# One computed order for the operations behind the softmax, on five queues

## The chip, the cores and the metric

The kernel runs on one core of a Trainium2 chip. The metric is the device time of one execution in microseconds (us); the kernel before takes 1281.55 us, the median of three runs (1279.1 to 1284.47). TensorE does the matrix products (PE; PEld is its weight load), VectorE (DVE) and ScalarE (ACT) work elementwise, GpSimd (POOL) does a little elementwise work, and SyncE (SP) issues the transfers. Each engine works through a queue of its own in a fixed order, and an instruction waits there for results of other engines.

## The reference

Channel attention over 6016 tokens of 256 channels is followed by two feed-forward networks. In short:

```
qn, kn = q / norm over tokens, k / norm over tokens
a = softmax(kn^T qn / tau)                  # 256 x 256
x = v @ a                                   # 6016 x 256
h = x @ w_in                                # network 1, 2048 wide
g = h where h >= 1; 0 where h <= -1; else (h + 1)^2 / 4
x = g @ w_out
xn = x / sqrt(mean(x^2) + 1e-6) * rms_g     # network 2, 1536 wide
out = (silu(xn @ w_gate) * (xn @ w_val)) @ w_out2
```

q, k and v are float32. The five weight matrices arrive as 64-bit floats.

## The kernel before

**Stages.** First q and k are read, their scores are summed up on TensorE, and the softmax gives the 256 x 256 matrix a. It is multiplied into w_in (`product_a`, four parts of 512 columns), so that network 1 works on v directly. Behind the softmax the 6016 tokens are treated as twelve tiles in six pairs: ten tiles of 512 tokens and two of 448. A pair goes through network 1 and later through network 2, in the order 1(0), 1(1), 2(0), 1(2), 2(1), 1(3), 2(2), 1(4), 2(3), 1(5), 2(4), 2(5), where 1(q) is network 1 of pair q.

**Precision.** Each operand of a product is split in a high part (h) and the rest (l), a ScalarE copy and a VectorE subtraction, and a product is three matmuls: high by high, low by high, high by low.

**Network 1.** For a tile t and a slice f of 128 of the 2048 columns, `emit_A` issues six matmuls into a PSUM tile h, `start_g` and `finish_g` turn it into gh and gl (three ScalarE and two VectorE instructions), and `block_B` adds it to the result y with six matmuls. A pair has 32 such blocks. `norm` and `combine` then normalize y, with two small matmuls into ms for each tile, and make the seven operands for network 2.

**Network 2.** The two tiles of a pair and the two halves of the channels form a 2 x 2 block product, done with seven products instead of eight. A group p covers 256 of the 1536 columns: seven products with w_gate (PSUM tiles gx, gz, gy), seven with w_val (vx, vz, vy), three matmuls each. Four products of a set go into the same accumulator, gx or vx; after the first three, ScalarE copies the sum so far out (ga, gc, gu and va, vc, vu, line 773) before the next product adds to it, and VectorE adds gz, gy, vz or vy to the copies (line 778). After the fourth, the sum is used straight from PSUM: ScalarE takes the Silu of the gate part (812), VectorE multiplies (818), uh and ul are split off, and `block_D` multiplies them with w_out2 into o. D is put off by one group: eight units of three matmuls of the group before are mixed in. A group thus has 22 units of three matmuls. `GROUP` is the order of units in it, written by hand: g, v and d stand for the next product of each set and a unit of D. There are four PSUM tiles for h, ms and the products, and two larger ones for y and o.

**Weights.** A 64-bit weight tile is read (wide), narrowed to float32 by bit operations on VectorE and ScalarE (`narrow`: clamp 223, shift 228 or 230, sign 234, rescale 238, join 242), and split. For w_in that serves `product_a`; w_out, w_gate, w_val and w_out2 are stored converted in DRAM (kept) and read again for each pair (wo, gw, vw, wd). For w_gate and w_val the seven weight combinations are formed, four of them by GpSimd (279), split by ScalarE (282) and VectorE (284). There are 34 such conversions; they run beside network 1 of pairs 0 and 1, so many steps after each block (`convert`, `pump`). Three tiles hold gw and vw.

**What sets the order.** The program is traced in loop order; a scheduler then places the instructions of each engine after estimated times, with priorities given in the code (`tc.high_priority`). TensorE's order behind the first 32 blocks is held as traced (`in_order(ENG.PE)`, line 941). Buffers come from pools that hand out the oldest free tile. `network_1` starts the norms of the pair before (task steps, two after each block); `network_2` starts the v tiles for a later pair. `store` transposes o and issues four stores for each half tile on SyncE (870).

## Time and profile before

| | |
|---|---|
| median of three runs | 1281.55 us (1279.1 to 1284.47) |
| the profiled execution's own time | 1281.39 us |
| its span, first to last instruction | 1279.6 us |
| TensorE busy | 1165.7 us, 4950 matmuls |
| VectorE busy | 850.1 us, 1311 instructions |
| ScalarE busy | 763.4 us, 1325 instructions |
| GpSimd busy | 80.1 us |
| granted TensorE clock, mean share of full | 0.985 |

The page gives the totals of one profiled execution; views of its trace give the busy time of each engine in any stretch, the instructions in order of time, and for each wait the instruction that ended it. The ends of matmuls are modelled, and matmuls overlap, so their start times tell more than their durations. Idle time of an engine that nothing waits for costs nothing.

### The profile page before, as it was taken

How to read it: one execution, taken by the hardware profiler on the slowest of the kernel's cores; microseconds unless marked ns; L12 is line 12 of the kernel's file. 1: busy time of each engine (PE TensorE's matmuls, PEld its weight loads, DVE VectorE, ACT ScalarE, POOL GpSimd, SP SyncE). 2: the span in 40 equal slices, each digit the busy share in tenths (PEclk: the TensorE clock that was granted, in tenths of full speed). 3: DMA queues.
4: the chain of work that ended last, by engine and by line, in shares of the span. 5: the costliest groups of instructions: out<-in, count | busy, mean ns of one | idle time of the engine just before them, and what ended most of it. 6: DMA issues, size and time to landing. Idle time of an engine off the chain costs nothing.

```text
span 1279.6 us, 13966 instructions
## 1 busy us (share of the span) xinstructions
PE 1165.7 (91%) x4950; PEld 927.0 (72%) x4950; DVE 850.1 (66%) x1311; ACT 763.4 (60%) x1325; POOL 80.1 (6%) x84
## 2 busy tenths in 40 slices
PE   8899987898999998999998999998999998889896
PEld 7677755676668786777786767786667897667775
DVE  6898889856558756557756556756556856765554
ACT  7687887774446665445675445666445765554442
POOL 0000334300001000000000000000000100100000
PEclk9989998999999999999999999999999999999998
DMA  9945786515334114344114444112334212433631
GB/s 355 223 138 156 279 295 238 158 54 134 142 137 122 50 50 117 138 148 132 42 50 119 148 141 115 66 50 91 107 144 138 80 50 91 148 120 132 179 133 29
DMA packets 138854, 167.65 MB, mean 131 GB/s; under 512 B 103712, under 2 KB 103712, under 8 KB 138784
## 3 DMA queue, kind: packets, MB, share of 16 engines
q1 hardware_dynamic: 138784, 166.75, 40.9%
q8 instruction: 39, 0.64, 0.2%
q14 instruction: 31, 0.25, 0.1%
HBM read 142.21 MB, written 24.51 MB: 130 GB/s over the span
## 4 chain that ended last, share of the span: by engine, by line
PE 48%; DVE 22%; ACT 18%; issue 4%; DMA 3%; POOL 2%; SPq 1%; DVEq 0%; ACTq 0%; POOLq 0%
PE o L851 12%; PE vx L760 8%; PE h L606 7%; PE gx L760 6%; PE y L649 6%; DVE g L617 5%; ACT gh L142 4%; ACT g L616 4%; PE gy L760 3%; ACT g L615 3%; DVE va L778 2%; PE vz L760 2%; DVE va L818 2%; DVE gl L139 2%; ACT vc L773 2%
## 5 line engine op out<-in xcount | busy, mean ns | idle before, releaser
L649 PE MATMUL y<-gh,wo 128*128 128x512 f32 (+1 forms) x768 | 237.7, 391 | 5.1 <-ACT gh L142 4.9
L142 ACT ACTIVATE gh<-g 128x512 fp32r<-128x512 f32 (+1 forms) x192 | 119.4, 622 | 121.9 <-DVE g L617 121.8
L139 DVE TENSOR_TENSOR gl<-g,gh 128x512 fp32r<-128x512 f32 (+1 forms) x192 | 134.5, 701 | 76.7 <-ACT gh L142 75.7
L851 PE MATMUL o<-uh,wd 128*128 128x512 f32 (+1 forms) x576 | 176.6, 388 | 0.0
L649 PEld LDWEIGHTS y<-gh,wo 128*128 128x128 f32 x768 | 144.5, 190 | 37.2 <-ACT gh L142 10.9
L617 DVE SCALAR_TENSOR_TENSOR g<-h,g 128x512 f32<-128x512 f32 (+1 forms) x192 | 129.6, 675 | 54.5 <-ACT g L616 53.4
L649 PE MATMUL y<-gl,wo 128*128 128x512 f32 (+1 forms) x384 | 151.5, 394 | 11.6 <-DVE gl L139 11.3
L606 PE MATMUL h<-vh,w1h 128*128 128x512 f32 (+1 forms) x384 | 150.6, 392 | 3.3 <-DVE g L617 3.0
L606 PE MATMUL h<-vl,w1h 128*128 128x512 f32 (+1 forms) x384 | 149.6, 390 | 0.0
L851 PEld LDWEIGHTS o<-uh,wd 128*128 128x128 f32 x576 | 108.6, 188 | 21.0
L616 ACT ACTIVATE g<-g 128x512 f32<-128x512 f32 (+1 forms) x192 | 119.5, 622 | 5.4
L606 PE MATMUL h<-vh,w1l 128*128 128x512 f32 (+1 forms) x384 | 119.1, 390 | 0.0
L851 PE MATMUL o<-ul,wd 128*128 128x512 f32 (+1 forms) x288 | 112.0, 389 | 0.0
L615 ACT ACTIVATE g<-h 128x512 f32<-128x512 f32 (+1 forms) x192 | 109.9, 572 | 0.7 <-PE h L606 0.5
L649 PEld LDWEIGHTS y<-gl,wo 128*128 128x128 f32 x384 | 72.6, 189 | 35.1 <-DVE gl L139 21.9
L606 PEld LDWEIGHTS h<-vh,w1h 128*128 128x128 f32 x384 | 73.0, 190 | 20.9 <-DVE g L617 6.1
L760 PE MATMUL vx<-xt,vw 128*128 128x512 f32 (+1 forms) x216 | 64.1, 405 | 24.9 <-ACT vc L773 24.9
L760 PE MATMUL gx<-xb,gw 128*128 128x512 f32 (+1 forms) x216 | 63.8, 404 | 24.1 <-ACT gu L773 24.1
L606 PEld LDWEIGHTS h<-vh,w1l 128*128 128x128 f32 x384 | 72.9, 190 | 14.1
L606 PEld LDWEIGHTS h<-vl,w1h 128*128 128x128 f32 x384 | 73.0, 190 | 13.8
L760 PE MATMUL gx<-xt,gw 128*128 128x512 f32 (+1 forms) x216 | 65.4, 412 | 15.4 <-ACT ga L773 14.2
L778 DVE TENSOR_TENSOR va<-vz,va 128x512 f32<-128x512 f32 (+1 forms) x36 | 24.5, 680 | 73.5 <-PE vz L760 70.5
(145 smaller groups left out, 1861.8 us busy)
## 6 DMA issues: line engine op xcount, KB each, us to landing
gw<-kept_g SPq DMA_DIRECT2D x36, 896.0 KB, 5.8
vw<-kept_v SPq DMA_DIRECT2D x36, 896.0 KB, 4.6
wo<-kept_wo SPq DMA_DIRECT2D x40, 512.0 KB, 3.3
wd<-kept_wd SPq DMA_DIRECT2D x36, 512.0 KB, 3.5
wide<-in_moe_w_out_dram SPq DMA_DIRECT2D x14, 512.0 KB, 4.5
vin<-in_v_dram SPq DMA_DIRECT2D x80, 64.0 KB, 2.9
out_dram<-ob SPq DMA_DIRECT2D x80, 64.0 KB, 2.0
qk<-in_q_dram SPq DMA_DIRECT2D x9, 512.0 KB, 10.2
```

The costliest lines, as they stand in the source:

```text
L139: return eng.tensor_tensor(out=dst_lo, in0=src, in1=hi.bitcast(F32), op=ALU.subtract)
L142: nc.scalar.activation(out=dst_hi, in_=src, func=AF.Copy)
L606: nc.tensor.matmul(ps[:, :n], w[:, c, f * P:(f + 1) * P], x[:, c, :n], start=(i == 0), stop=(i == len(terms) - 1),)
L615: nc.scalar.activation(out=r[:, :n], in_=ps[:, :n], func=AF.Relu, bias=0.5, scale=0.5)
L616: on_act = nc.scalar.activation(out=r[:, :n], in_=r[:, :n], func=AF.Square)
L617: on_dve = nc.vector.scalar_tensor_tensor(out=r[:, :n], in0=ps[:, :n], scalar=1.0, in1=r[:, :n], op0=ALU.max, op1=ALU.min)
L649: nc.tensor.matmul(y_ps[t][:, c, :n], w[:, h, cs], x[:, :n], start=(f == 0 and i == 0), stop=(f == NF1 - 1 and i == 2),)
L760: nc.tensor.matmul(ps[:, :n], w[:, h, a, :], x[:, p, :n], start=(start and i == 0), stop=(i == 2), skip_group_check=True,)
L773: nc.scalar.activation(out=d[:, :n], in_=ps[:, :n], func=AF.Copy)
L778: nc.vector.tensor_tensor(out=d[:, :n], in0=ps[:, :n], in1=d[:, :n], op=ALU.add)
L818: nc.vector.tensor_tensor(out=out[:, :n], in0=s[:, :n], in1=d[:, :n], op=ALU.mult)
L851: nc.tensor.matmul(o_ps[t][:, c, :n], w[:, h, cs], x[:, :n], start=(nth == 1 and i == 0), stop=(nth == NF2 and i == 2),)
```

## The change

What comes up to the softmax and the first part of `product_a` stays, apart from three weight tiles that are read right behind the first two v tiles. Everything behind it is no longer issued where it is traced. `op` records each operation with its engine, a cost and a latency written in the code (`pe`, `act`, `dve`, ...), a wanted time `at`, what it reads and writes, and which buffers it opens. A list scheduler then takes, again and again, the operation that can start first (ties by `at` less `urgent`), gives it free buffer slots by number, and issues it. The order in which it does so is held on all five engines, SyncE's queue included. The operations themselves are the same in kind and number.

The order of products in a set is now the accumulator's first, gz, the accumulator's second, gy's first, the accumulator's third, its fourth, gy's last (p1, p2, p6, p7, p5, p3, p4), and the last two are left over and mixed into the set that follows (`CHAIN`: c is the next product of this set, t one left over, d a unit of D). `norm` of a pair is wanted shortly after the end of its network 1, in the network-2 stage of the pair before; the conversions are spread up to the end of network 2 of pair 0. The last pair's stores are issued half by SyncE and half by ScalarE.

```diff
-GROUP = "g g d g g d v v g d v g d g v v d d v d d v".split()
+CHAIN = "ccttccddcdd"
+
+SLOTS = {"mm": 4, "yo": 2, "stage": 7, "op": 19, "rows": 4, "tmp": 20, "seven": 3}
...
+    ordered.enter_context(in_order(
+        ENG.PE, ENG.DVE, ENG.Activation, ENG.Pool, ENG.SP
+    ))
...
+    def op(eng, cost, fn, at, reads=(), writes=(), new=(), urgent=0.0):
+        o = Op()
+        o.eng, (o.occ, o.lat), o.fn, o.at, o.urgent = eng, cost, fn, at, urgent
+        o.uses = [(*u, False) if isinstance(u, tuple) else (u, 0, False) for u in reads]
+        o.uses += [(*u, True) if isinstance(u, tuple) else (u, 0, True) for u in writes]
+        o.new, o.seq = list(new), len(ops)
+        ops.append(o)
+
+    def pe(k, n):
+        t = k * (n / 2400 + 0.0133)
+        return t, t + LATE["PE"]
+
+    def act(n):
+        t = 0.075 + n * 0.00096
+        return t, t + LATE["ACT"]
+
+    def dve(n):
+        t = 0.06 + n * 0.00114
+        return t, t + LATE["DVE"]
...
+        return [p1, p2, p6, p7, p5, p3, p4]
...
+            def put(queue, some):
+                src = ob.t.rearrange("p (b i) -> p b i", i=32)
+                for a in some:
+                    queue.dma_start(out=dst[a, c], in_=src[32 * a:32 * a + 32, :n // 32, :])
+            if t // 2 < NPAIR - 1:
+                op("SP", dma(256, 4), lambda: put(nc.sync, range(4)), at, [ob])
+            else:
+                op("SP", dma(128, 2), lambda: put(nc.sync, range(2)), at, [ob])
+                op("ACT", dma(0, 2), lambda: put(nc.scalar, range(2, 4)), at, [ob])
...
+    def network_2(q):
+        before = ORDER[ORDER.index((2, q)) - 1]
+        at = end_at[1, q] + NORM_AT
+        while fill and (1, q) == before:
+            pop_fill(1)
+        for i in range(2):
+            norm(2 * q + i, at + i * NORM_GAP, STEP)
+        combine(q, max(at + NORM_GAP + 15 * STEP, phase_at[before] + 8), STEP)
...
+            for chain in sets:
+                fill.extend(pend)
+                pend.clear()
+                for what in CHAIN:
+                    if what == "d":
+                        pop_fill(1)
+                    elif what == "t":
+                        if tail:
+                            unit(us, tail.pop(0))
+                    else:
+                        unit(us, chain.pop(0))
+                tail.extend(chain)
...
+    while left:
+        best = None
+        for e in clock:
+            c = clock[e]
+            for o in pending[e]:
+                if best is not None and max(o.ready, c) > best[0][0]:
+                    continue
+                if o.at > front[0].at + REACH[e]:
+                    continue
+                t = may_start(o)
+                if t is None:
+                    continue
+                key = (t, o.ready + SURE[e] > t, o.at - o.urgent, o.seq)
+                if best is None or key < best[0]:
+                    best = key, o
...
+        o.fn()
```

What this does to the order shows in three places. First, TensorE in network 2 of pair 2, the middle of group 3, before: vx2_3 is the accumulator of the w_val set, gx2_3 and gy2_3 are tiles of the w_gate set, o4 and o5 take D of the group before.

```order
L760 MATMUL vy2_3_5965<-xt3_2_5078,vw3_5877 128x512 x3
L760 MATMUL gx2_3_5910<-xb22_2_5110,gw3_5801 128x512 x3
L851 MATMUL o5_5719<-uh2_2_01_5873,wd2_5758 128x512 x2
L851 MATMUL o5_5719<-ul2_2_01_5874,wd2_5758 128x512
L760 MATMUL gy2_3_5927<-xt4_2_5107,gw3_5801 128x512 x3
L760 MATMUL vx2_3_5939<-xt2_2_5081,vw3_5877 128x512 x3
L760 MATMUL vx2_3_5939<-xt1_2_5050,vw3_5877 128x512 x3
L851 MATMUL o5_5719<-uh2_2_11_5891,wd2_5758 128x512 x2
L851 MATMUL o5_5719<-ul2_2_11_5892,wd2_5758 128x512
```

The same place in the change:

```order
L855 MATMUL vz2_3_5994<-xb21_2_4626,vw3_5876 128x512 x3
L855 MATMUL gx2_3_5917<-xb22_2_4763,gw3_5810 128x512 x3
L855 MATMUL vx2_3_5970<-xt2_2_4697,vw3_5876 128x512 x3
L855 MATMUL gy2_3_5950<-xt4_2_4753,gw3_5810 128x512 x3
L855 MATMUL vy2_3_6014<-xt3_2_4727,vw3_5876 128x512 x3
L948 MATMUL o5_5693<-uh2_2_11_5963,wd2_5514 128x512 x2
L948 MATMUL o5_5693<-ul2_2_11_5979,wd2_5514 128x512
```

Before, the products with xt2 and xt1 into vx2_3 follow each other. In the change gy2_3, vy2_3 and the D units stand behind the one with xt2, and its next, with xt1, comes after the o5 pair has stood there a second time.

Second, VectorE in network 2 of pair 2, before, from the first split behind the adds of group 2 on: ga, gc, gu, va, vc and vu are the copies, s a Silu, ul the low parts.

```order
L139 TENSOR_TENSOR ul2_2_10_5831<-va2_2_5822,uh2_2_10_5830 128x512
L778 TENSOR_TENSOR gu2_2_5837<-gy2_2_5806,gu2_2_5837 128x512
L778 TENSOR_TENSOR gc2_2_5813<-gy2_2_5806,gc2_2_5813 128x512
L778 TENSOR_TENSOR vu2_2_5869<-vy2_2_5844,vu2_2_5869 128x512
L818 TENSOR_TENSOR vu2_2_5869<-gu2_2_5837,vu2_2_5869 128x512
L818 TENSOR_TENSOR s2_2_11_5851<-s2_2_11_5851,vx2_2_5818 128x512
L139 TENSOR_TENSOR ul2_2_01_5874<-vu2_2_5869,uh2_2_01_5873 128x512
L139 TENSOR_TENSOR ul2_2_11_5892<-s2_2_11_5851,uh2_2_11_5891 128x512
L778 TENSOR_TENSOR vc2_2_5864<-vy2_2_5844,vc2_2_5864 128x512
L818 TENSOR_TENSOR vc2_2_5864<-gc2_2_5813,vc2_2_5864 128x512
L139 TENSOR_TENSOR ul2_2_00_5907<-vc2_2_5864,uh2_2_00_5906 128x512
L778 TENSOR_TENSOR ga2_3_5914<-gz2_3_5916,ga2_3_5914 128x512
```

The change, in group 1 of the same pair: sa, sb, sl and ms belong to the norms of tiles 6 and 7 (pair 3), vt8 to the v tiles of pair 4.

```order
L143 TENSOR_TENSOR sl6_5684<-sa6_5590,sh6_5662 128x512
L771 TENSOR_TENSOR sb7_5691<-x7_5622 128x512
L143 TENSOR_TENSOR ul2_0_11_5699<-s2_0_11_5600,uh2_0_11_5682 128x512
L773 TENSOR_TENSOR sa7_5631<-sa7_5631,sb7_5691 128x512
L568 STREAM_TRANSPOSE vt8_0_5713<-vin8_5220 128x512
L868 TENSOR_TENSOR gu2_1_5705<-gy2_1_5664,gu2_1_5705 128x512
L786 STREAM_TRANSPOSE sb6_5620<-ms6_5707 128x512
L143 TENSOR_TENSOR ul2_0_00_5727<-vc2_0_5585,uh2_0_00_5697 128x512
L143 TENSOR_TENSOR sl7_5740<-sa7_5631,sh7_5719 128x512
L568 STREAM_TRANSPOSE vt8_1_5745<-vin8_5220 128x512
L868 TENSOR_TENSOR va2_1_5689<-vz2_1_5736,va2_1_5689 128x512
L868 TENSOR_TENSOR gc2_1_5675<-gy2_1_5664,gc2_1_5675 128x512
```

Before, 14 instructions stand from ga2_2 to ga2_3, all of the group. In the change 24 stand from ga2_1 to ga2_2, and 24 more to ga2_3, ten of each for other pairs' norms and v tiles.

Third, SyncE at the end of the kernel, before: ob is a transposed part of the result.

```order
L372 DMA gw5_9936<-kept_g5_127 128x1792
L372 DMA vw5_10012<-kept_v5_128 128x1792
L870 DMA out_dram<-ob11_0_10178 32x14x32 x4
L870 DMA out_dram<-ob11_1_10184 32x14x32 x4
L870 DMA out_dram<-ob10_0_10196 32x14x32 x4
L870 DMA out_dram<-ob10_1_10202 32x14x32 x4
```

In the change, SyncE and behind it ScalarE:

```order
L668 DMA gw5_9919<-kept_g5_470 128x1792
L668 DMA vw5_9988<-kept_v5_471 128x1792
L965 DMA out_dram<-ob11_0_10169 32x14x32 x2
L965 DMA out_dram<-ob11_1_10174 32x14x32 x2
L965 DMA out_dram<-ob10_0_10181 32x14x32 x2
L965 DMA out_dram<-ob10_1_10185 32x14x32 x2
```

```order
L924 ACTIVATE uh5_5_00_10156<-vc5_5_10103 128x448
L965 DMA out_dram<-ob11_0_10169 32x14x32 x2
L965 DMA out_dram<-ob11_1_10174 32x14x32 x2
L965 DMA out_dram<-ob10_0_10181 32x14x32 x2
L965 DMA out_dram<-ob10_1_10185 32x14x32 x2
```

Of the 16 last stores eight have moved to ScalarE's queue, behind its last uh.

## Rows read from the trace of the kernel before

**Rows 1.** The page's head and its totals of busy time by engine

```profile
span 1279.6 us, 13966 instructions
...
PE 1165.7 (91%) x4950; PEld 927.0 (72%) x4950; DVE 850.1 (66%) x1311; ACT 763.4 (60%) x1325; POOL 80.1 (6%) x84
```

**Rows 2.** The chain of waits, network 1 (start us, us, what)

```profile
443.08 1.36 PE h L606 x6
...
1041.39 1.24 PE h L606 x6
```

**Rows 3.** Busy us by stage: length, PE, PEld, DVE, ACT, POOL, clock, DMA, GB/s

```profile
55.80:278.50 222.70, 198.22 (x792) 149.68 (x791) 191.05 (x300) 175.52 (x299) 48.19 (x58) 0.96 0.59 195
278.50:387.40 108.90, 96.10 (x392) 72.96 (x392) 62.01 (x95) 54.58 (x94) 0.00 (x0) 0.98 0.40 128
387.40:978.30 590.90, 554.61 (x2353) 438.73 (x2353) 370.11 (x568) 340.57 (x591) 18.69 (x12) 0.99 0.33 103
978.30:1269.20 290.90, 268.69 (x1209) 224.78 (x1207) 184.23 (x302) 155.34 (x289) 12.50 (x8) 0.99 0.34 110
1269.20:1279.60 10.40, 0.00 (x1) 0.00 (x0) 1.19 (x3) 0.00 (x0) 0.00 (x0) 0.69 0.56 88
```

**Rows 4.** The same view, one group of network 2, pair 0

```profile
314.50:331.70 17.20, 15.83 (x67) 12.16 (x67) 9.36 (x14) 8.04 (x14) 0.00 (x0) 1.00 0.42 139
```

**Rows 5.** Who waited for whom, TensorE: us in total, times, longest us

```profile
PE vx L760 <- ACT vc L773: 24.9, 36, 0.7
PE gx L760 <- ACT gu L773: 24.1, 34, 1.1
PE gx L760 <- ACT ga L773: 14.2, 9, 2.2
```

**Rows 6.** Timeline, one group of pair 4 (start us, us, [idle before <-releaser])

```profile
1125.75 0.85 PE L760 MATMUL vx<-xt,vw 128*128 128x512 f32 x3
...
1126.70 0.60 ACT L773 ACTIVATE vc<-vx 128x512 f32<-128x512 f32 x1 [0.33 <-PE vx L760]
...
1127.35 0.96 PE L760 MATMUL vx<-xt,vw 128*128 128x512 f32 x3 [0.75 <-ACT vc L773]
...
1138.02 0.84 PE L760 MATMUL gx<-xt,gw 128*128 128x512 f32 x3
...
1139.74 0.63 ACT L142 ACTIVATE uh<-va 128x512 fp32r<-128x512 f32 x1 [1.55 <-DVE va L818]
...
1140.27 0.58 ACT L773 ACTIVATE gu<-gx 128x512 f32<-128x512 f32 x1
...
1140.90 0.96 PE L760 MATMUL gx<-xb,gw 128*128 128x512 f32 x3 [0.69 <-ACT gu L773]
```

**Rows 7.** Groups of instructions, VectorE: count, busy us, mean ns, idle before

```profile
L778 DVE TENSOR_TENSOR va<-vz,va 128x512 f32<-128x512 f32 (+1 forms) x36 | 24.5, 680 | 73.5 <-PE vz L760 70.5 <-ACT va L773 2.9
...
L234 DVE SCALAR_TENSOR_TENSOR wide<-wide 128x512 uint32<-128x512 uint32 x34 | 23.6, 697 | 0.2
...
L223 DVE TENSOR_SCALAR wide<-wide 128x512 f32<-128x512 f32 x34 | 15.3, 462 | 2.2 <-DMA wide<-in_moe_w_out_dram 1.6 <-DMA wide<-in_moe_w_gate_dram 0.7
...
L284 DVE TENSOR_TENSOR fg<-fg,hg 128x896 fp32r<-128x896 f32 x6 | 6.9, 1144 | 1.5 <-ACT hg L282 1.4
```

**Rows 8.** Busy time in the densest conversion stretch

```profile
160.00:240.00 80.00, 63.52 (x233) 44.81 (x232) 73.25 (x109) 63.25 (x108) 34.63 (x40) 0.94 0.74 254
```

**Rows 9.** Timeline, the end of the span

```profile
1268.03 2.39 DVE L867 STREAM_TRANSPOSE ob<-o 128x448 f32<-128x448 f32 x4 [1.04 <-PE o L851]
1268.70 8.40 SPq L870 DMA_DIRECT2D out_dram<-ob  x16
```

**Rows 10.** SyncE's longest wait, and the weight loads (KB, us to landing)

```profile
SPq L372 <- PE gy L760: 330.8, 35, 14.2
...
gw<-kept_g SPq DMA_DIRECT2D x36, 896.0 KB, 5.8
vw<-kept_v SPq DMA_DIRECT2D x36, 896.0 KB, 4.6
```

1234 lines of the change are left out of this document (672 added, 562 removed).

## Prediction

> **What bounds the kernel now.** I read the page's totals first, then the busy time by stage, then one group of the second network, then who waited for whom, and last the end of the span. The totals [rows 1]: TensorE is busy for 1165.7 of 1279.6 us with 4950 matmuls, so it is the engine to feed, and at most 114 us of it are idle. A matmul of 512 columns costs 0.2267 us when they follow each other without a gap, since six take 1.36 us; with 448 columns six take 1.24 us, 0.207 each [rows 2]. That gives a floor for each stage of [rows 3], counted from the program (a pair's first network has 384 matmuls, its second network 6 groups of 66, its norms 4):
> - 55.8 to 278.5 us, pairs 0 and 1 through network 1 beside the weight conversions: 792 matmuls, 792 x 0.2267 = 179.5 us; it takes 222.7.
> - 278.5 to 387.4, network 2 of pair 0: 396 x 0.2267 = 89.8; it takes 108.9.
> - 387.4 to 978.3, three cycles of network 1 and network 2: each 784 x 0.2267 = 177.7, in all 533.1; they take 590.9.
> - 978.3 to 1269.2, the last network 1 (448 columns), network 2 of pairs 4 and 5: 79.4 + 89.8 + 0.9 + 81.8 = 251.9; it takes 290.9.
> - 1269.2 to the end, no matmul runs: 10.4 us.
>
> In network 2 the loss has a form. One group of 66 matmuls takes 17.20 us, TensorE at full clock, while VectorE is busy for 9.36 and ScalarE for 8.04 of it [rows 4]: neither is short. The floor is 66 x 0.2267 = 14.96, so 2.24 us are lost in each group, about 80 us in 36 (the smaller groups lose a little less). The wait list names them: TensorE waits 24.9 us for the copy vc, 24.1 for gu, 14.2 for ga, each one a copy that ScalarE makes out of the accumulator (gx or vx) that the next product adds to [rows 5]. The idle times do not hold the whole stall, since the first matmuls behind each one run longer. The timeline shows why [rows 6]: the product into vx starts at 1125.75, its copy runs from 1126.70 to 1127.30, and the next product into vx starts at 1127.35, although nothing but itself stood between. So from the start of a product to the start of the next into the same tile it takes at least 1.60 us. The other pair shows a queue: gx starts at 1138.02, but its copy gu only at 1140.27, because ScalarE had waited 1.55 us at uh for a VectorE result; gx goes on at 1140.90, 2.88 us after the first.
>
> **The change, part by part.** *Products in another order.* The instruction order tells how far apart two products into one accumulator stand. Before, of the 216 such pairs 36 follow each other directly and 71 more have only two units (six matmuls, 1.36 us) between. In the change none follows directly, 9 have six matmuls and one five, all others eight or more, most of them 9 to 12 (2.0 to 2.7 us; start to start 2.7 to 3.4). The first excerpt of the section on the change shows the vx pair that stood together now apart by gy, vy and two units of D. Against the 1.60 us that leaves 1.1 us or more for a queue on ScalarE; the queued case above needed 2.88 and would still wait for some tenths where only nine matmuls lie between. I take the stall as gone where VectorE has room, 14.96 us a group. Less cannot be had, since the matmuls are the same in number, so the bounds are 14.96 and 17.20.
>
> *Norms, combines and v preparations moved.* What the change adds to network 2 is VectorE work. The second excerpt shows it: between the adds that begin two groups stood 14 VectorE instructions; in the second and third group of a middle pair there are now 24 each, with norm and transpose steps. At 0.68 us [rows 7] that is 48 x 0.68 = 32.6 us of work, in two groups whose TensorE floor with a norm's four matmuls is 30.8. VectorE is never busy all the time: in the densest 80 us of the trace it reaches 73.25, 91.6% [rows 8]. So these two groups need 32.6 / 0.916 = 35.6 us, 4.8 over the floor. This work was in network 1 before, where it was hidden (VectorE has two instructions of 0.68 us in a block of 2.72), so the change pays it back in a tighter place. What waits there: the add of gz frees the PSUM tile that gy needs, and everything queued on VectorE in front of that add delays TensorE. A cycle then costs 177.7 + 4.8, and I allow 2 us for the turns between the networks, where queues empty: 184.5, three of them 553.5 (from 590.9). Bounds 533.1 and 590.9.
>
> *Conversions spread.* Before, 160 to 240 us is VectorE's [rows 8], with TensorE at 63.5 of 80. Of what must be done on VectorE before network 2 starts, 191.05 us [rows 3], the change moves five conversions behind it: five sign steps and five joins at 0.697 us, four clamps at 0.462, two subtractions at 1.144 [rows 7], 11 us in all. 180 us at 91.6% are 196.5; with 3.5 for the time until the first block's results are there, 200 (from 222.7). Bounds: TensorE's 180 and the old 222.7. The conversions come back in network 2 of pair 0, together with the norms of pair 1: 72 VectorE instructions in groups 2 to 4, 49.0 us, at 91.6% 53.5, against 44.9 of TensorE and 0.9 of norms: 8 over the floor. 89.8 + 0.9 + 8 + 1 for the turn = 99.7 (from 108.9); bounds 90.7 and 108.9.
>
> *Last pairs.* Floor 251.9, 4.8 for pair 4's norms and combine, 3 for the last group, which has no next group to fill its gaps: 259.7 (from 290.9).
>
> *Last stores on two queues.* After the last matmul the end is issue: 16 stores take SyncE 8.40 us, 0.525 each, beginning when the first of four transposes is done [rows 9]. Eight on each of two queues take 4.2, so the tail is 6.2 (from 10.4). ScalarE's issue time is not in this trace; were it twice SyncE's, its eight would take 8.4 and nothing would be won; a loss I leave out, since SyncE's own eight run beside them. I take SyncE's 0.525; the four copies ahead of them on ScalarE are done by then. The Trainium skill says in "DMA: Bandwidth & Descriptors", section "Issuing engines are not separate DMA queues", that a second issuing engine saves the sequencer's issue time only, since the same DMA engines move the data; by that rule, too, the gain is bounded by these 8.4 us.
>
> *Fixed slots and a fixed SyncE order.* The bytes are the same. I cost it at nothing: SyncE waits in all 330.8 us for gy products to free a weight tile, and the loads behind that land in 5.8 (gw) and 4.6 us (vw) [rows 10]. In the change gy's last product is the 16th of 22 units, 10.9 us into its group, and the vw load that waits for it is used first 5.4 us into the next: 9.5 us for a 4.6 us load. That is the cover; without it TensorE waits in each group.
>
> **Sum** against the profiled execution: 55.8 (unchanged up to the first block) + 200 + 99.7 + 553.5 + 259.7 + 6.2 = 1174.9 of span; that execution took 1281.39 with a span of 1279.6, 1.8 around it, and the median shown is 1281.55, the same within noise. 1176.7, so 1177 us.
>
> **The rivals.**
> 1. *TensorE bound throughout.* VectorE's lag in the dense groups could be absorbed by tiles that are free anyway. All stages at their floors: 55.8 + 180 + 90.7 + 533.1 + 251.9 + 6.2 + 1.8 = 1119.5; with part of the excess, about 1140. For it: VectorE has 5.6 us to spare in each other group. Against: four PSUM tiles hold back less than two units.
> 2. *Half of it lost to the fixed queues.* The order was computed with 0.644 us for a 512-column VectorE instruction and 0.567 for a ScalarE one (numbers in the code), the trace has 0.68 [rows 7] and 0.58 to 0.63 [rows 6]. If an instruction that comes late holds its whole queue, the three middle stages lose half of their 77.8 us: 1177 + 38.9 = 1216.
> 3. *The groups stay at 17.2 us.* The four accumulating PSUM tiles and their number are the same. If the recurring stall is one of tiles and not of the copy, gy and the next gx wait as long in the new order, 36 x 2.2 = 79 us come back: 1256. Against it: [rows 5] name copies of the accumulator itself, not the adds that free a tile. The Trainium skill, "Perfetto Trace Analysis", section "Optimization Strategy", reads a gap that repeats on the saturated engine as a possible lack of SBUF or PSUM for the next tile; it would put its weight here.
> 4. *Nothing measurable*: 3, and the dense groups give away what the conversions bring: 1275 to 1288.
> 5. *Slower: weights come late.* Place: the vw load behind gy on SyncE's fixed queue. It decides from the point where a load takes over 9.5 us from the freed tile to landing; each us over costs 36. From 12.4 us on the kernel is slower than before (104 / 36 = 2.9); at 13.5, 36 x 4.0 = 144: 1321. For it: one queue in fixed order, where the stores wait for transposes in front of loads. Against: DMA engines are busy for only 0.42 of a group [rows 4] and the load takes less than half of that.
>
> **How the numbers follow.** The forecast holds 0.56 (its own range 1150 to 1200), rival 1 0.11, rival 2 0.17, rival 3 0.06, rival 4 0.03, rival 5 0.07. The range, 1136 to 1240, takes in 1 and 2 and leaves out 3 to 5 and the far end of 1. A measurement here can tell about 0.5% (6.4 us) from no change. Faster: 0.56 + 0.11 + 0.17 + 0.06 = 0.90; within it 0.03; slower 0.07.
>
> **What would show it.** Right: groups four and five of a pair at 15.0 to 15.3 us, the second and third at 16.5 to 18; the copies vc, gu and ga gone from the top of TensorE's waits, VectorE's adds in their place; VectorE above 85% in network 2; the first product of network 2 near 256 us; the stretch behind the last matmul near 6 us. Wrong: quiet groups above 16 us (rival 2 or 3; the first if ScalarE or VectorE stands idle in front of a late instruction, the second if TensorE waits for adds there), or TensorE waiting for DMA in network 2 (rival 5).

## The result, and the profile after

The changed kernel takes 1134.4 us (median of four runs, 1133.6 to 1134.8) where the kernel before takes 1280.3: 0.886 of its time, 95% interval 0.883 to 0.888. The forecast was 1177 with a range from 1136, so it lies 42.6 us too high and the range ends 1.6 us above what came. Rival 1, TensorE bound throughout (1119.5 to about 1140), describes the run.

The page's totals of the profiled execution (busy us, share of the span, instructions), which answer to [rows 1]:

```profile
span 1133.1 us, 13952 instructions
...
PE 1109.2 (98%) x4950; PEld 930.7 (82%) x4950; DVE 820.0 (72%) x1311; ACT 749.6 (66%) x1325; POOL 86.4 (8%) x84
```

Then busy time by stretch: six stages that end where those of [rows 3] end (the first block, the first product of network 2, network 1 of pair 2, the last network 1, the last matmul), and groups two, three and four of pair 1 in network 2. Columns as in [rows 3].

```profile
0.00:62.50 62.50, 49.51 (x210) 41.67 (x211) 45.74 (x57) 37.99 (x53) 0.68 (x6) 0.95 0.78 265
62.50:242.30 179.80, 179.08 (x786) 146.83 (x785) 169.72 (x279) 160.68 (x289) 44.38 (x48) 1.00 0.64 209
242.30:331.80 89.50, 89.50 (x397) 74.00 (x396) 78.87 (x127) 63.20 (x113) 14.16 (x14) 1.00 0.60 192
331.80:865.20 533.40, 533.40 (x2353) 441.42 (x2352) 356.73 (x568) 337.68 (x592) 21.10 (x12) 1.00 0.39 116
865.20:1124.10 258.90, 257.40 (x1211) 226.82 (x1209) 167.44 (x281) 150.08 (x281) 6.09 (x4) 1.00 0.41 130
1124.10:1133.10 9.00, 0.34 (x2) 0.00 (x0) 1.50 (x3) 0.00 (x0) 0.00 (x0) 0.66 0.75 102
433.79:449.75 15.96, 15.96 (x72) 13.13 (x70) 15.27 (x26) 11.50 (x21) 4.09 (x4) 1.00 0.50 180
449.75:464.72 14.97, 14.97 (x68) 12.39 (x66) 14.95 (x26) 8.28 (x16) 2.82 (x1) 1.00 0.53 179
464.72:479.68 14.96, 14.96 (x68) 12.39 (x66) 10.81 (x18) 8.47 (x15) 0.00 (x0) 1.00 0.45 156
```

From 62.5 us to the last matmul TensorE stands idle for 2.2 us in all. In the third row from the end VectorE is busy for 15.27 of 15.96 us (that group holds a norm's four matmuls more), in the next for 14.95 of 14.97, and TensorE does not wait. The list of TensorE's waits, of [rows 5]'s view, has lost all the copies, and no add has come in their place:

```profile
PE a_ps L457 <- ACT s_sb L451: 6.9, 2, 5.3
PE s_ps L304 <- DMA qk<-in_k_dram: 5.8, 2, 4.3
PE o L948 <- DVE ul L143: 1.5, 1, 1.5
PE h L708 <- ACT w1h L414: 0.3, 1, 0.3
```

VectorE's timeline in the full group (start us, us) shows why they fit: each is recorded as 0.69 us long, but they start 0.60 to 0.61 us apart.

```profile
456.41 0.69 DVE L920 TENSOR_TENSOR vc<-gc,vc 128x512 f32<-128x512 f32 x1
457.01 0.69 DVE L868 TENSOR_TENSOR gu<-gy,gu 128x512 f32<-128x512 f32 x1
457.61 0.68 DVE L868 TENSOR_TENSOR va<-vz,va 128x512 f32<-128x512 f32 x1
458.21 0.68 DVE L143 TENSOR_TENSOR ul<-vu,uh 128x512 fp32r<-128x512 f32 x1
```

One stage went the other way. The first block starts at 62.57 us, before at 56.06. Of these 6.5 us 4.5 are a later start of `product_a` (57.69 against 53.19), and 2.0 are its slower matmuls: it takes 4.88 us, before 2.87, at a granted clock of 0.55 in place of 1.00. TensorE's timeline around it ([idle before <-releaser]):

```profile
55.19 0.62 PE L457 MATMUL a_ps<-ident,s_sb 128*128 128x128 f32 x2 [5.33 <-ACT s_sb L451]
57.35 0.69 PE L457 MATMUL a_ps<-ident,s_sb 128*128 128x128 f32 x2 [1.55 <-ACT s_sb L451]
57.69 2.06 PE L405 MATMUL w_ps<-wi,ah 128*128 128x512 f32 x4
```

and VectorE's, where the conversions of the tiles named soon stand between the softmax's instructions and wait for their DMAs:

```profile
52.35 0.43 DVE L206 TENSOR_SCALAR soon<-soon 128x512 f32<-128x512 f32 x1 [0.96 <-DMA soon<-in_moe_w_in_dram]
52.69 0.48 DVE L445 SCALAR_TENSOR_TENSOR s_sb<-s_ps,rk,rq 128x256 f32<-128x256 f32 x1
53.65 0.43 DVE L206 TENSOR_SCALAR soon<-soon 128x512 f32<-128x512 f32 x1 [0.48 <-DMA soon<-in_moe_w_out_dram]
53.99 0.41 DVE L449 TENSOR_REDUCE mx<-s_sb 128x1 f32<-128x256 f32 x1
```

The end: eight stores on each queue, which answer to [rows 9]. The DMA engines' share behind the last matmul rose from 0.56 [rows 3] to 0.75 in the stage table.

```profile
1123.91 5.30 SPq L965 DMA_DIRECT2D out_dram<-ob  x8
1123.92 5.39 ACTq L965 DMA_DIRECT2D out_dram<-ob  x8
```

### The profile page after: what moved, and what is told of

Its sections match the earlier page's. It is cut to its first block, busy times and chain, and to the rows that moved or that the text cites. A ratio compares the mean times of both kernels' runs of the same rounds, so it can differ in the third digit from the quotient of the medians.

```text
span 1133.1 us, 13952 instructions
## 1 busy us (share of the span) xinstructions
PE 1109.2 (98%) x4950; PEld 930.7 (82%) x4950; DVE 820.0 (72%) x1311; ACT 749.6 (66%) x1325; POOL 86.4 (8%) x84
## 4 chain that ended last, share of the span: by engine, by line
PE 93%; DMA 4%; DVE 1%; SPq 1%; ACT 0%; issue 0%; DVEq 0%; ACTq 0%
PE y L742 23%; PE h L708 22%; PE o L948 17%; PE vx L855 9%; PE gx L855 9%; PE gy L855 4%; PE vy L855 4%; PE vz L855 2%; PE gz L855 2%; DMA qk<-in_k_dram 1%; DMA wide<-in_moe_w_in_dram 1%; DMA qk<-in_q_dram 1%; PE w_ps L682 1%; SPq L180 1%; DMA soon<-in_moe_w_out_dram 1%; PE w_ps L405 0%
## 5 line engine op out<-in xcount | busy, mean ns | idle before, releaser
L742 PE MATMUL y<-gh,wo 128*128 128x512 f32 (+1 forms) x768 | 233.5, 385 | 0.0
L717 ACT ACTIVATE g<-h 128x512 f32<-128x512 f32 (+1 forms) x192 | 112.8, 587 | 121.5 <-PE h L708 121.3
L708 PE MATMUL h<-vh,w1h 128*128 128x512 f32 (+1 forms) x384 | 148.1, 386 | 0.3 <-ACT w1h L414 0.3
L742 PE MATMUL y<-gl,wo 128*128 128x512 f32 (+1 forms) x384 | 148.0, 385 | 0.1
L143 DVE TENSOR_TENSOR gl<-g,gh 128x512 fp32r<-128x512 f32 (+1 forms) x192 | 129.2, 678 | 7.4 <-ACT gh L725 7.1
L725 ACT ACTIVATE gh<-g 128x512 fp32r<-128x512 f32 (+1 forms) x192 | 117.0, 611 | 6.8 <-DVE g L722 6.8
L948 PEld LDWEIGHTS o<-ul,wd 128*128 128x128 f32 x288 | 54.1, 188 | 12.1 <-DVE ul L143 1.9
L855 PE MATMUL gy<-xt,gw 128*128 128x512 f32 (+1 forms) x216 | 60.0, 386 | 0.0
L855 PE MATMUL vx<-xt,vw 128*128 128x512 f32 (+1 forms) x216 | 60.0, 386 | 0.0
L855 PE MATMUL gx<-xb,gw 128*128 128x512 f32 (+1 forms) x216 | 60.0, 386 | 0.0
## 6 DMA issues: line engine op xcount, KB each, us to landing
qk<-in_q_dram SPq DMA_DIRECT2D x9, 512.0 KB, 10.2
qk<-in_k_dram SPq DMA_DIRECT2D x9, 512.0 KB, 10.2
```

The source lines that it names most:

```text
L143: return eng.tensor_tensor(out=dst_lo, in0=src, in1=hi.bitcast(F32), op=ALU.subtract)
L708: nc.tensor.matmul(ps.t[:, :n], w[:, c, f * P:(f + 1) * P], x[:, c, :n], start=(i == 0), stop=(i == len(terms) - 1),)
L717: op("ACT", act(n), lambda: nc.scalar.activation(out=r.t[:, :n], in_=ps.t[:, :n], func=AF.Relu, bias=0.5, scale=0.5), at, [ps], [r], [r])
L725: op("ACT", act(n), lambda: nc.scalar.activation(out=gh.t[:, :n], in_=r.t[:, :n], func=AF.Copy), at, [r], [gh], [gh])
L742: nc.tensor.matmul(y.t[:, c, :n], w.t[:, f % 2, h, cs], x[:, :n], start=(f == 0 and i == 0), stop=(f == NF1 - 1 and i == 2),)
L855: nc.tensor.matmul(ps.t[:, :n], w.t[:, h, a, :], b.t[:, e, :n], start=(start and i == 0), stop=(i == 2), skip_group_check=True,)
```

## Experiments on the price of VectorE's work

All times are medians of four runs; the changed kernel is 1134.4.

**norms_net1.** The norms of pairs 1 to 4 go back into network 1.

```diff
-        at = end_at[1, q] + NORM_AT
+        at = max(end_at[1, q], phase_at[before] if before[0] == 1 else 0.0) + NORM_AT
```

> The changed kernel with the norms of pairs 1 to 4 back in network 1, where the kernel before had them: the second and third group of a middle pair then have 17 or 18 VectorE instructions in place of 24 to 26. Theory: VectorE's full groups cost TensorE nothing (there VectorE is busy for 14.95 of 14.97 us and TensorE has no gap), so nothing can be won: 1134 within 2 us. Rival, the prediction's: a full VectorE delays the adds and with them TensorE, so freeing it gives back up to 4.8 us in each of three cycles: down to 1120.

Measured 1135.4 us. By the instruction order groups two and three then hold 18 and 17 VectorE instructions in place of 24 each. A cycle from first product to first product is 177.9 us as against 177.8: a full VectorE had cost TensorE nothing.

**hid4, hid8.** Two (four) instructions that the planner doesn't know of in front of each add of gz and vz.

```diff
+            def go():
+                for _ in range(2 if name == "a" else 0):      # 4 in hid8
+                    nc.vector.tensor_tensor(out=spare, in0=w1h[:, 0, :TOK].bitcast(F32),
+                        in1=w1h[:, 1, :TOK].bitcast(F32), op=ALU.add)
+                nc.vector.tensor_tensor(out=d.t[:, :n], in0=b.t[:, :n], in1=d.t[:, :n], op=ALU.add)
-            op("DVE", dve(n), lambda: nc.vector.tensor_tensor(
-                out=d.t[:, :n], in0=b.t[:, :n], in1=d.t[:, :n], op=ALU.add),
-                at, [b], [d], urgent=20)
+            op("DVE", dve(n), go, at, [b], [d], urgent=20)
```

> The changed kernel with four more VectorE instructions in each group of network 2 that the planner doesn't know of: two 512-column adds into a spare tile directly in front of each add of gz and of vz. The two full groups of a middle pair then have 28 each. Theory A (a VectorE instruction costs the 0.60 us from start to start that back-to-back ones show, and 56 x 0.60 = 33.6 us in 30.9 of TensorE is over by 2.7): 2.7 us in each of three cycles, some 5 in pair 0's network 2 and 3 in pair 4's, in all about 16 over: 1150. Theory B, the prediction's price (0.68 / 0.916 = 0.742 us each): 56 x 0.742 = 41.6, over by 10.7 in each cycle and by as much in pairs 0 and 4: 1134 + 53 = 1187. Theory C (each delayed add holds TensorE by the two instructions in front of it, however idle VectorE is): 72 x 1.2 = 86: 1220.

> As hid4 with four instructions in front of each of these adds, eight more in a group: 32 in a full group, 22 to 24 in the others. Theory A (0.60 us each, other groups still fit in 14.96 us): 64 x 0.60 = 38.4 in 30.9, over by 7.5 in each of three cycles, 12 in pair 0's, 7 in pair 4's: 1134 + 42 = 1176. Theory B (0.742 us each): 64 x 0.742 = 47.5, over by 16.6, and 24 x 0.742 = 17.8 in 14.96 over by 2.8 in the other groups: 3 x (16.6 + 8.4) + 45: 1250. Theory C: 72 x 2.4 = 173: 1307.

Measured 1164.1 and 1260.5 us, that is 29.7 and 126.1 more. Theory A gave half and a third of that. The two full groups of pair 1 in hid4:

```profile
442.70:459.70 17.00, 16.52 (x72) 12.98 (x70) 16.74 (x29) 11.79 (x21) 3.79 (x2) 1.00 0.48 174
459.70:477.21 17.51, 15.64 (x68) 12.15 (x66) 17.44 (x30) 8.79 (x15) 3.12 (x2) 1.00 0.42 145
```

VectorE is busy for 98 to 99.6% with 29 and 30 instructions, 0.58 us each in the mean (some are the short copies): its capacity is theory A's, and theory B's 91.6% is passed. What A left out is in the waits, gy and vy behind the late adds: 9.6 + 7.0 us in hid4, 46.6 + 30.6 in hid8, also in groups whose VectorE has room. Theory B's 1250 for hid8 came near by the wrong way. Part of hid8's loss is a lower granted clock (0.98 in the cycle shown below, 1.00 in the changed kernel). What the place alone costs shows in a quiet group of pair 1, first hid4 (two instructions in front of each add), then hid8 (four):

```profile
492.92:507.88 14.96, 14.96 (x67) 12.39 (x66) 11.39 (x19) 8.55 (x16) 0.00 (x0) 1.00 0.48 163
522.22:539.18 16.96, 15.56 (x67) 12.23 (x66) 14.14 (x23) 8.63 (x16) 0.00 (x0) 1.00 0.42 140
```

The changed kernel's quiet group takes 14.96 too. So two instructions (1.2 us) in front of each add cost nothing here, four (2.4 us) cost 2.0 us: an add has some slack, and what goes beyond it is paid. That is why theory C, which charged the whole delay, was too high.

**hid8b, extra8.** The same 288 instructions: in hid8b behind the add in place of in front of it, in extra8 as operations that the planner knows.

```diff
+            for i in range(8):                                # extra8, once in each group
+                e = Buf("tmp", f"e{q}_{p}_{i}")
+                op("DVE", dve(TOK), lambda e=e: nc.vector.tensor_tensor(out=e.t, ..., op=ALU.add),
+                    now + i * 14.0 / 8, [], [e], [e])
```

> The changed kernel with the same 288 VectorE instructions as hid8 (eight 512-column adds into spare tiles for each group of network 2), but known to the planner and with no place of their own: it puts at most 24 or 25 in a group of a middle pair and the rest (some 27 of 40 a cycle) into network 1. Theory (work on VectorE costs TensorE nothing as long as no stretch holds more than its 0.60 us each, and no add stands behind it): 1134 to 1142, against hid8's 1260. Rival, the prediction's price (0.742 us each, so 24 of them need 17.8 us): four groups of 24 in each cycle over by 2.8 each: 1134 + 3 x 11 + some 20 in pairs 0, 4 and 5 = 1187 or more.

> hid8 with its four unplanned instructions directly behind each add of gz and vz in place of in front of it. Theory (hid8 lost 126 us to two things: full groups whose 32 VectorE instructions need 19.5 us or more, and adds that come 2.4 us late in every group): the first part stays, two groups over by 4 to 5 us in each of five pairs, some 45; of the second part most goes: 1134 + 45 to 80 = 1180 to 1215. Rival (the sum of the work alone decides): 1260 as hid8.

Measured 1143.9 (extra8, 2 us above its theory's range) and 1234.5 us (hid8b; above what was expected, since whatever stands behind the added work then comes late: gy and vy for gu and vu, o for ul, vx for s). One whole cycle of each, first the changed kernel, then extra8, hid8b and hid8:

```profile
420.19:598.00 177.81, 177.81 (x786) 147.14 (x784) 119.08 (x189) 112.47 (x198) 6.91 (x4) 1.00 0.40 116
```

```profile
429.76:607.93 178.17, 178.08 (x785) 147.08 (x784) 146.56 (x237) 111.73 (x198) 6.91 (x4) 1.00 0.40 116
```

```profile
445.57:640.17 194.60, 184.14 (x785) 146.94 (x784) 149.08 (x237) 112.79 (x198) 6.91 (x4) 0.99 0.37 106
```

```profile
447.81:646.82 199.01, 184.26 (x786) 148.61 (x785) 149.25 (x237) 113.49 (x198) 6.92 (x4) 0.98 0.35 103
```

In each of the last three VectorE runs 237 instructions in the cycle, 48 more than the first. Planned they cost 0.4 us, unplanned 17 to 21. Some ten of these are the amount: the two full groups, which hold 24 each in extra8, hold 32 each in hid8b and hid8 and take 41.4 and 40.8 us together, as against 30.9, with VectorE busy for 95 to 99% of them. The rest is place. The other 9 us of extra8 come from network 2 of pair 0, which takes 89.4 us in the changed kernel. There the last conversions stand beside the added work and VectorE is full, and that is paid too:

```profile
242.31:342.72 100.41, 94.84 (x401) 75.40 (x400) 97.26 (x159) 61.44 (x109) 15.01 (x14) 0.98 0.54 171
```

So more work on VectorE costs TensorE nothing as long as VectorE has time for it in that stretch and none of it holds up an instruction that TensorE waits for.

**early_conv.** Three more of the late conversions are made before network 2.

```diff
-    late[i] = (phase_at[2, 0] * first + (c[0] - phase_at[2, 0] * first) * (i + 1) / len(late),) + c[1:]
+    late[i] = (phase_at[2, 0] * (first + (last - first) * (i + 1) / len(late)),) + c[1:]
```

> The changed kernel with the due times of the late conversions drawn in, so that 33 of 34 joins stand before the first add of network 2 in place of 30: twelve more VectorE instructions before network 2. Theory (0.60 us each, 7 us, and VectorE has 9.5 us of idle time between 62.5 and 242 us): 1134 to 1138. Rival, the prediction's price (VectorE can't pass 91.6%): (169.7 + 7.2) / 0.916 = 193 us in place of 180: 1147.

Measured 1140.5 us, between the two, nearer to the theory:

```profile
62.86:247.88 185.02, 180.99 (x784) 148.02 (x785) 178.08 (x291) 165.99 (x299) 53.63 (x57) 0.99 0.66 219
```

VectorE reaches 96% here, and the stage grows by 5.2 us, 3.63 of them in one wait of TensorE for g. So it is worth 6 us in the changed kernel that these three stand behind the first add of network 2. What spreading the conversions as a whole is worth was not measured.

## Experiments on where the gain came from

**strict_new, strict_old.** TensorE takes its units in written order; strict_old also has the order of products of the kernel before.

```diff
-REACH = {"PE": 8.0, ...}
+REACH = {"PE": 0.0, ...}
-        return [p1, p2, p6, p7, p5, p3, p4]          # strict_old alone, from here
+        return [p1, p2, p7, p6, p5, p3, p4]
-CHAIN = "ccttccddcdd"
+GROUP = "g g d g g d v v g d v g d g v v d d v d d v".split()
...
+            for what in GROUP:
...
```

> The changed kernel, but TensorE takes its units strictly in the order in which they are written, and that order is the one of the kernel before: of the 216 pairs of products into gx or vx 31 stand directly behind each other and 72 have six matmuls between, as before; the computed queues of the four other engines, planned buffers and stores stay. Theory (the distance of the products is what the 80 us of network 2 were): the groups go back to 16.5 to 17.2 us, 36 x 1.5 to 2.2 us: 1190 to 1213. Theory with a prompt ScalarE: the computed queues put the copy in front, so only the directly adjacent pairs lose 1.60 - 0.68 = 0.92 us each, 31 x 0.92 = 29: 1163. Rival (the fixed, planned queues, not the distance, made the gain): 1134 to 1142.

> The control of strict_old: TensorE strictly in written order, with the changed kernel's order of products (six pairs with three matmuls between, six with six, all others nine or more). Theory: the planner's freedom to move TensorE's units is worth little, so 1134 to 1140 (six pairs with 1.60 us needed and 1.36 there cost next to nothing). Rival (the freedom to swap units is what fills the gaps): over 1150.

Measured 1185.0 and 1149.9 us. A quiet group of strict_old, and what TensorE waits for there:

```profile
482.51:498.46 15.95, 15.26 (x68) 12.31 (x66) 8.98 (x14) 8.28 (x14) 0.00 (x0) 1.00 0.41 148
```

```profile
PE vx L855 <- ACT vc L863: 22.4, 36, 0.7
```

The same group of strict_new:

```profile
455.55:470.51 14.96, 14.96 (x68) 12.39 (x66) 13.68 (x23) 8.72 (x17) 1.08 (x1) 1.00 0.46 158
```

So the one pair of products per group that follow each other directly costs 0.99 us, near the 1.60 - 0.68 = 0.92 of [rows 6], and 35 us in the kernel. The planner's freedom to move TensorE's units is worth another 15.5, which strict_new's theory had put at little. The 72 pairs with six matmuls between cost nothing here: the list of strict_old's waits names vc alone among the copies. Theory one laid most or all of the 2.24 us of a group to the distance; it was less than half of them.

**b_spread.** The other way round: the kernel before with its GROUP order changed alone.

```diff
-GROUP = "g g d g g d v v g d v g d g v v d d v d d v".split()
+GROUP = "g g d g g d v v g d v d g v g d d v d d v v".split()
```

> The kernel before with another GROUP order alone: 5 in place of 36 pairs of products into gx or vx stand directly behind each other, 31 in place of 71 have six matmuls between, the rest nine or more. Theory (an adjacent pair costs 1.0 us, as strict_old's groups of 15.95 against 14.96 us show, and the rest of a group's 2.24 us is late queues of ScalarE and VectorE, which stay): 31 x 1.0 = 31 less, 1250. Rival 1 (the distance is the whole 2.24 us of a group): 80 less, 1200. Rival 2 (the scheduler's queues are as late in the new order, and take it all back): 1275 to 1282.

Measured 1229.4 us against 1283.0 for the kernel before beside it, 53.6 less: between theory and rival 1. Its quiet group:

```profile
518.15:534.17 16.02, 15.59 (x67) 12.23 (x66) 9.15 (x15) 8.05 (x15) 0.00 (x0) 1.00 0.43 148
```

17.20 us [rows 4] went to 16.02; the other 1.06 over 14.96 stays, and its waits name the first product's copy ga on ScalarE (17.4 us in all). That this is a late queue follows from strict_old, where all these pairs have nine matmuls between them, as here, and wait for nothing. More than the 31 us of the theory came because the new order also takes gu's pair from six matmuls between to nine: TensorE's waits for gu fall from 24.1 us [rows 5] to 1.3. So with a late ScalarE six are too few, with a prompt one (strict_old) they are enough.

**free_two, free_all.** No fixed order on VectorE and ScalarE, or on any of the five engines; the program is still written in the computed order.

```diff
     ordered.enter_context(in_order(
-        ENG.PE, ENG.DVE, ENG.Activation, ENG.Pool, ENG.SP
+        ENG.PE, ENG.Pool, ENG.SP          # free_all: without these lines altogether
     ))
```

> The changed kernel without the fixed order on VectorE and ScalarE: their instructions are written in the computed order, but the scheduler that orders the kernel before is free to move them. TensorE, GpSimd and SyncE keep the fixed order. Theory (TensorE's order and the planned buffers carry the gain, VectorE and ScalarE follow it as their inputs come): 1134 to 1150. Rival 1 (the two queues' order is most of the 96 us that lie between the kernel before and strict_old): over 1180. Rival 2 (a fixed queue costs time where an instruction comes late, so freedom gains): under 1132.

> The changed kernel with no fixed order on any of the five queues behind the softmax: the computed order is only the order in which the program is written, and the scheduler of the kernel before orders all engines. Theory (the scheduler undoes much of it, since it now moves six-matmul distances and the norms' places by its own costs): 1150 to 1200. Rival (the written order alone is what the change brings): 1134 to 1142.

Measured 1154.5 us (free_two, above its theory's range and far below rival 1) and 1154.6 us (free_all, in its theory's). The fixed order of the queues is worth 20 us, and freeing the other three engines loses no more than VectorE and ScalarE do; the computed order as it is written keeps 126 of the 146 us even where the old scheduler may move everything. In free_two 8.2 us are lost ahead of network 2 (first product at 250.5, not 242.4; 2.1 of them ahead of the first block), 7.9 in the cycle that begins with pair 0's, and 2.4 in each of the next two cycles, in the full group three (17.3 us); quiet groups take 14.95 to 14.97.

## Experiments on the start and the end

**soon_a, soon_b, soon_c.** The early conversions are queued behind the last softmax instruction (soon_a) or, on VectorE alone, behind its last reciprocal (soon_b; ScalarE's stay where they were). In soon_c they stand as in soon_a, and the planner knows that the engines come free late.

```diff
+        behind = {"ACT": v_hi(1, 1).ins, "DVE": v_lo(1, 1).ins}   # soon_b: {"DVE": last_rs.ins}
...
+        if o.eng in behind:
+            with tc.issue_after(behind.pop(o.eng)):
+                o.fn()
...
-    clock = {e: 0.0 for e in ("PE", "ACT", "DVE", "POOL", "SP")}
+    clock = {"PE": 0.0, "ACT": 2.0, "DVE": 3.0, "POOL": 0.0, "SP": 0.0}   # soon_c
```

> The changed kernel with one edit: the conversions of the three weight tiles loaded early are queued on VectorE and ScalarE behind the last softmax instruction, where the changed kernel had them between the softmax's instructions. Theory: in the changed kernel these instructions wait for their DMAs at the head of VectorE's fixed queue and hold the softmax, which is the whole of the 6.5 us that the first block of network 1 is late (62.57 against 56.06 us): the first block returns to 56 us, the stage behind it keeps its 180 us, and the time is 1134.4 - 6.5 = 1128. Rival: VectorE is busy for 94% of the stage behind, so conversions that begin some 9 us later make TensorE wait there for weights: the first block is at 56 us but the first product of network 2 stays near 242, and the time near 1134.

> As soon_a, but VectorE may begin the early conversions behind the last reciprocal of the row sums, so some of them stand before the evictions of the first product and the last preparations of v. Theory (the queue's place is all that matters): the softmax is free of them too, first block near 57 us (seven instructions of 0.42 to 0.68 us now stand before the first eviction, which in the kernel before had 0.5 us to spare), time 1128 to 1131. Rival (the stage behind needs the conversions early): this one is faster than soon_a by 1 to 3 us.

> As soon_a, and the planner is told that VectorE comes free 3 us and ScalarE 2 us behind its zero, so it puts the first block's VectorE instruction in front of some of the early conversions. Theory (in soon_a TensorE lost 2.22 us at 65.67 us because that instruction stood behind ten of the conversions): no wait there, first product of network 2 near 238 us, 1128 to 1129. Rival (then a weight comes late in its place): 1131 to 1133, with TensorE waiting for wo or w1l before 80 us.

Measured 1132.7, 1131.0 and 1130.9 us. The theory on the place was right: in soon_a the softmax runs through, `product_a` starts at 53.33 us (before 53.19), and the first block is at 57.48 us, 1.4 late, since the granted clock falls to the lower level here too (0.50 from 52 to 54 us). In soon_b the time came out as expected, but not the reason: the first block is at 60.17 us, because ScalarE's step of an early conversion still waits for its DMA in front of the softmax's exponential.

```profile
52.31 0.66 ACT L213 ACTIVATE soon<-soon 128x512 uint32<-128x512 uint32 x1 [1.77 <-DMA soon<-in_moe_w_in_dram]
```

The rival was right on the price: first products of network 2 came at 240.1, 240.1 and 239.4 us, not 236 to 238. In soon_a TensorE waits behind the late conversions,

```profile
65.67 0.79 PE L707 MATMUL h<-vh,w1h 128*128 128x512 f32 x1 [2.22 <-DVE g L721]
```

and in soon_c, with that mended, for the weight itself:

```profile
70.62 0.50 PE L741 MATMUL y<-gh,wo 128*128 128x512 f32 x1 [1.12 <-DVE wo L143]
```

So 2.3 to 3.0 of the 6.5 us lost at the start are had back up to network 2. The medians gained 1.7 to 3.5 us, but part of what these profiles gain lies elsewhere, in the groups of the last pair: 13.38 us where the changed kernel's take 13.64, and 13.37 in norms_net1 too, whose start was left as it is. The same group in the changed kernel, soon_c and norms_net1:

```profile
1075.40:1089.04 13.64, 13.64 (x68) 12.39 (x66) 8.31 (x15) 7.42 (x14) 0.00 (x0) 1.00 0.49 166
1072.59:1085.97 13.38, 13.38 (x68) 12.40 (x67) 8.29 (x15) 7.41 (x14) 0.00 (x0) 1.00 0.51 165
1077.82:1091.19 13.37, 13.37 (x67) 12.39 (x67) 8.27 (x15) 7.42 (x14) 0.00 (x0) 1.00 0.49 169
```

Five such groups make 1.3 us; their cause stays open.

**one_queue.** All sixteen last stores on SyncE.

```diff
-                op("SP", dma(128, 2), lambda: put(nc.sync, range(2)), at, [ob])
-                op("ACT", dma(0, 2), lambda: put(nc.scalar, range(2, 4)), at, [ob])
+                op("SP", dma(256, 4), lambda: put(nc.sync, range(4)), at, [ob])
```

> The changed kernel with all sixteen last stores on SyncE's queue again. Theory: on two queues the end is no longer issue but the movement of the data (the DMA engines are busy for 0.95 to 1.04 of the time from 1124.5 to 1131 us), so the second queue bought only 10.4 - 9.0 = 1.4 us: time 1135 to 1136.5, stretch behind the last matmul 10 to 10.5 us. Rival, the prediction's own: issue sets the end, 16 x 0.525 = 8.4 against 5.4 us measured: 3 us longer, 1137.4.

Measured 1135.5 us, 1.1 more: the theory.

```profile
1123.59 8.39 SPq L965 DMA_DIRECT2D out_dram<-ob  x16
```

Sixteen issues on one queue take 0.52 us each, on two queues 0.66 to 0.67 each, side by side. Behind the last matmul issue ends 3.0 us earlier with two, but the span only 1.75 in these two profiles and 1.1 in the medians: the transfers end last. The DMA engines' busy share shows it too: with one queue it stays at 0.71 to 0.74 while the stores are issued, with two it is full, 1.03 to 1.07 from 1126 to 1131 us. The Trainium skill, "DMA: Bandwidth & Descriptors", section "Issuing engines are not separate DMA queues", says that all such transfers run on the same 16 DMA engines and that a second issuing engine saves the sequencer's time only; the trace agrees, with these numbers.

**best.** soon_c, and the last group's uh and ul marked urgent for the planner.

```diff
+            soon = 20 if (q, p) == (NPAIR - 1, NF2 // 2 - 1) else 0
-                ... at, [out], [uh], [uh])
+                ... at, [out], [uh], [uh], urgent=soon)
-                ... at, [out, uh], [ul])
+                ... at, [out, uh], [ul], urgent=soon)
```

> soon_c, and in the last group ScalarE's and VectorE's uh and ul are marked urgent for the planner, so that the first ul stands in front of vc's add and product on VectorE. Theory (the 1.50 us for which TensorE waits for ul at 1120.87 us in the changed kernel is that place in the queue): 1.5 less than soon_c, 1126.5 to 1127.5. Rival (vc's own chain then ends later, and the last block waits for it): as soon_c.

Measured 1129.2 us (1128.6 to 1130.4), 1.8 less than soon_c and 5.2 less than the changed kernel: 0.881 of the kernel before, interval 0.880 to 0.883. The theory was right in size (its range lay lower, since it built on a soon_c of 1128). The wait shrank and moved behind vc's chain, as the rival had it, so both had a part:

```profile
1118.16 0.47 PE L948 MATMUL o<-ul,wd 128*128 128x448 f32 x1 [0.55 <-DVE ul L143]
```

## Why the prediction was wrong

By its own sum, measured against forecast: start 62.5 for 55.8 (+6.7), conversion stage 179.8 for 200 (-20.2), network 2 of pair 0 89.5 for 99.7 (-10.2), three cycles 533.4 for 553.5 (-20.1), last pairs 258.9 for 259.7 (-0.8), end 9.0 for 6.2 (+2.8). Together -41.8, which is 1174.9 against 1133.1.

- *The failed step is the price of VectorE's work*, "48 x 0.68 = 32.6 us", "32.6 / 0.916 = 35.6 us, 4.8 over the floor", and the same 91.6% in the conversion stage. Both factors were wrong. 0.68 us is how long an instruction is recorded; the next starts after 0.60 [the timeline of the full group above], so 48 need 28.8 us, under TensorE's 30.8. And 91.6% was the share of a stretch in which VectorE stood idle for 6.7 us, 5.5 of them waiting for ScalarE's results by the list of its waits, and no ceiling: it reaches 99.9% in the changed kernel. In the conversion stage the work itself was put too high as well: 180 us were counted and 169.7 came, part of the difference being eight steps of the early tiles that now run ahead of the first block. With 0.60 and no ceiling the terms for VectorE (16.5 in the conversion stage, 8 in pair 0, 4.8 in each cycle and in the last pairs, in all 43.7) come to nothing, and the forecast to 1133, in rival 1's range. That this nearly is the time measured is luck: 13.5 us allowed for the first block, the turns and the last group were not needed, and 16.5 us at the start, at the end and in the last pairs (below) were missing. norms_net1 shows that the full groups cost nothing, extra8 that 48 more instructions in a middle cycle don't either, hid4 that 29 and 30 instructions take 17.0 and 17.5 us at a busy VectorE. The Trainium skill, "Perfetto Trace Analysis", section "DVE / Act Engine Instruction (TENSOR_ADD, Activation, etc)", says that the reported time ends with the acknowledged write, and that the next instruction may begin its prefetch before that, when the execution ends; the trace agrees (0.69 and 0.60).
- *"What waits there: the add of gz ..."* names the right place. hid8 shows it: with the adds late, TensorE waits 77 us for them. In the changed kernel no wait for an add is listed. That the planned order is the reason, since it keeps other work away from an add that is due, is argued from hid4 and hid8 and not shown by itself.
- *The products' distance* held in direction and in the groups' time (14.96 us as forecast), but not in its reasons: directly adjacent pairs make 0.99 of the 2.24 us [strict_old], the rest is late copies on ScalarE [strict_old, b_spread], which the prediction had seen in the case of 2.88 us and not weighed.
- *Two turns per cycle* (2 us) and 3 us for the last group were unneeded; 1.5 us stands at the end, one ul behind vc's add on VectorE, which is rival 2's mechanism in its only instance there.
- *The start, "unchanged"*: the prediction counts five conversions that move behind the stage, but gives the early tiles' conversions no place and no price. They stand in the softmax's VectorE queue and wait for DMAs at its head, which costs 4.5 us, and the lower clock behind that wait another 2.0; soon_a shows the place.
- *Last pairs* came out right by two errors: the floor of 251.9 left out units of network 2 of pair 3 that run behind the first block (TensorE is busy for 257.4 there, with 1211 matmuls where 1180 were counted, 7 us; [rows 3] has 1209 in the same stage), and the 7.8 us of VectorE that had been added didn't come.
- *The end* was priced by issue alone; each issue costs 0.66 us with two queues, and the transfers end later.

Rival 3, the tiles, is refuted: groups take 14.96 us with the same four accumulating tiles. So what the Trainium skill, "Perfetto Trace Analysis", section "Optimization Strategy", gives as a possible reason of a repeating gap, too little SBUF or PSUM for the next tile, was not this case. Rival 5 did not show: the list above has no wait for a weight's transfer.

The conversion stage, 222.7 us before and 179.8 in the change, gained 43 us, and that is only in part taken apart. TensorE stood idle there for 24.5 us, and the waits name results of VectorE and ScalarE, for network 1 and for the norms (sh, sl) that stood in it:

```profile
PE y L649 <- DVE gl L139: 8.4, 13, 1.5
PE ms L688 <- ACT sh L142: 4.5, 2, 3.1
PE y L649 <- ACT gh L142: 3.7, 7, 0.8
PE h L606 <- DVE g L617: 3.0, 2, 1.8
PE ms L689 <- DVE sl L139: 2.8, 2, 1.6
```

The granted clock was 0.96 there. The fixed queues are worth 6 to 7 us of the gain (the stage takes 185.9 us in free_two and 187.0 in free_all), and early_conv shows 6. No run tells how the other 30 divide between the written order, the norms' new place and the spread of the conversions.

## What to carry to other kernels

Price work on VectorE by the distance from start to start of instructions that follow each other, not by their recorded length, and don't take the busiest stretch of a stalled kernel for a ceiling. An engine that is full costs nothing as long as its work fits into the stretch and no instruction that the bound engine waits for stands too far behind others that could come later; where it does, the delay beyond its slack is paid. When early work is put into a fixed queue, look at what stands behind its first wait for a DMA.

## What the runs showed of the hardware

- In the changed kernel VectorE starts 512-column FP32 instructions every 0.60 us with 0.69 recorded, and stays busy for 14.95 of 14.97 us.
- From 67.8 to 1119.4 us the changed kernel's trace names no wait of TensorE at all, at a granted clock of 1.00. After the 5.33 us wait in the softmax four 512-column matmuls took 2.06 us, and the granted clock from 56.0 to 62.5 us was 0.53, mostly the lower of its two levels; six such matmuls take 1.36 us [rows 2]. So a pause of the softmax can be paid a second time behind it. The pause's length alone does not decide it: after 2.43 us the same four matmuls took 2.07 in soon_a, 1.22 in soon_c and 1.19 in the kernel before. In soon_c the lower level came a little later (four matmuls at 55.43 us took 1.91), in the kernel before the clock stayed at 1.00 up to 64 us. Each is one profiled execution.

```profile
56.00:62.50 6.50, 5.15 (x14) 4.14 (x15) 4.80 (x13) 1.94 (x5) 0.00 (x0) 0.53 0.01 3
```
